# Selective scan with a gated MLP on one core: decay rows loaded at the head of two queues, B weighed by GpSimd in block 0, fewer and wider dummy matmuls

## The chip, the cores and the metric

The kernel runs on one core of a Trainium2 chip: TensorE (PE) for matmuls, VectorE (DVE), ScalarE (ACT) and GpSimd (POOL) for elementwise work, and SyncE (SP), which here only issues transfers; ACT issues some too. The metric is the device time of one execution in microseconds, as the median over runs. A profile is of one such execution; its span runs from the first to the last instruction.

## The reference, cut to what matters

```python
# x (4, 8, 768, 32), a (4, 8, 768) decays, B and C (4, 8, 768, 16)
log_a = np.log(np.clip(a, 1e-06, 1.0))
for c in range(nc):                      # chunks of the sequence
    cum = np.cumsum(la, axis=-1)
    L = np.exp(cum[:, :, :, None] - cum[:, :, None, :]) * causal
    y_intra = ((C @ B^T) * L) @ x
    y_inter = (C @ state) * np.exp(cum)[..., None]
    y[:, :, sl] = y_intra + y_inter
    state = decay_full * state + sum_j (B_j * decay_from_j) x_j
h = y as (3072, 256)
out = (silu(h @ w_gate) * (h @ w_val)) @ w_out      # d_ff = 1536
```

## The kernel before

The 768 steps of the sequence are cut into six blocks `k` of 128 steps, each of two pieces `q` of 64. A block holds all four batches `b`, so 512 tokens. In each block the scan part gives `y`, and the MLP part gives twelve gate and value products `gv` (one weight tile `wg0` to `wg11` each), then the sums `po` with `wo0` to `wo5`. The MLP's products are most of PE's work.

Products of decays within a piece are made by a scan along the free axis on DVE, which writes `L` (per source step) and `E` (per state). B is weighed by a column of `L` (`weigh_b`), C by `E` (`weigh_c`). `S` are the scores C B, `mix` multiplies them by `L`, `st` are the sums that make the new states, which ACT takes apart into `T`. `values` gives the first part of `y`, `carried` adds what comes from the state of the piece before.

Block 0 is the head. Its decays come as rows (`load_rows`): for the pieces, the partitions 32 b and 32 b + 1 of the tile `rows` hold batch `b`; 8 further rows hold the decays for `E`. `clip_rows` clips them, PE spreads a row over partitions by a matmul with a selector from `cs` (`spread`, output `a`, in two halves of the heads), and DVE scans that (`scan_spread`). The decays of the other blocks are loaded into `all`, clipped by POOL (`clip_all`), written back to memory as `clipped`, and read from there, broadcast, block by block. `dj` and `dn` are the added terms of the scans. `idle` issues dummy matmuls on the tile `unit`, with output `rest`.

Weights come as 64-bit words. DVE and ACT turn each tile into a float32 value (steps magnitude, range, rest, shift, sign, round) and then into a high and a low part. In block 0 `gv` uses the float32 values; in the others it uses the parts.

The order of instructions is not written out by hand: `Plan` is a small list scheduler. Each operation is added with an engine and a cost, a rank (its due time), what it needs, and the buffers it takes; `Plan.order` simulates the engines, and at each step issues what can start first, with the lowest rank. `follow` chains operations into a fixed order. Every engine runs its instructions strictly in the order issued. `IDLE` lists the ranks of five groups of dummies, `IDLE_AFTER` what each group follows. Transfers issued from SP and ACT are given eight completion semaphores in turn, so an issue can wait for an earlier transfer that had the same one.

All helpers that issue instructions pass through one line, 190, so the profile's lines say little, and the tile names are what to read.

Of the kernel before, what the change touches and what calls it, by code (L numbers as in the profile page):

```python
# [23 lines left out]
K = P // Q  # L24
# [19 lines left out]
class Plan:  # L44
# [156 lines left out]
def scan_moe_kernel(ctx: ExitStack, tc, aj, an, bc, xb, wgv, wo, cst, sel, out):  # L201
    nc = tc.nc
    PSUM = bass.MemoryType.PSUM
    te, ve, se, ge, sp = (
        Ordered(tc, e) for e in (nc.tensor, nc.vector, nc.scalar, nc.gpsimd, nc.sync)
    )
# [4 lines left out]
    const = pool("const", 1)  # L211
# [3 lines left out]
    raw = pool("raw", RAW)  # L215
    dram = pool("dram", 1, space=bass.MemoryType.DRAM)
    ps_mm = pool("ps_mm", 4, space=PSUM)
    ps_at = pool("ps_at", 4, space=PSUM)

    cs = const.tile([P, CST], F32, name="cs")  # L220
    eye, hm, blk = cs[:, 0:W], cs[:, W : W + 2], cs[:, W + 2 : W + 2 + 2 * D]
    pick = cs[:, CST - P :]
    dj = const.tile([P, H, W], F32, name="dj")
    dn = const.tile([P, BATCH * K, W], F32, name="dn")
    unit = const.tile([P, P], BF16, name="unit")
    pick_n = const.tile([H, P], F32, name="pick_n")

    const.tile([P, 48], F32, name="gap")
# [1 line left out]
    clipped = dram.tile([2, P, NA * W], F32, name="clipped")  # L230
    bl = [dict(y={}) for _ in range(NB)]
# [8 lines left out]
    def load_rows():  # L240

        t = moe.tile([P, 2, T + 32], F32, tag="xl", name="rows")
        t = bl[0]["rows"] = t[:, :, : H * W]
        ve.memset(t[:, 0], 1.0)
        to = t[:, 0].rearrange("(b r) c -> b r c", b=BATCH)
        for q in range(K):
            sp.dma_start(to[:, q], aj[0, q].rearrange("(b c) -> b c", b=BATCH))
        sp.dma_start(t[:H, 1], an[0])

    def load_aj(k):  # L250
# [34 lines left out]
    def load_xb(k):  # L285
        t = bl[k]["xb"] = att.tile([P, BATCH, DM + P], F32, tag="xb", name=f"xb{k}")
        bl[k]["x"], bl[k]["Bj"] = t[:, :, :DM], t[:, :, DM:]
        (sp if k else se).dma_start(t, xb[k])
# [11 lines left out]
        ve.tensor_tensor_scan(t, t, d, 0.0, ALU.mult, ALU.add)  # L300

    def clip_rows(i):
        t = bl[0]["rows"][:H, 1] if i else bl[0]["rows"][:, 0]
        clip(t.rearrange("p (g t) -> p g t", t=W)[:, :, 1:])

    HALF = H // 2 * W
# [1 line left out]
    def first(b, i):  # L308
        return b < BATCH and not i
# [37 lines left out]
            else:  # L347
                ve.tensor_scalar(t[:, :, h], bl[k]["C"], hm[:, h : h + 1], None, ALU.mult)

    def weigh_b(k, b):  # L350

        t = bl[k]["Bj"].rearrange("p b (h n) -> p b h n", n=N)[:, b]
        L = bl[k]["L"].rearrange("p (b h) t -> p b h t", h=H)[:, b, :, Q:]
        ve.tensor_tensor(out=t, in0=t, in1=L.to_broadcast([P, H, N]), op=ALU.mult)

    def weigh_c(k):
        t = bl[k]["C"].rearrange("p b (q i) -> p b q i", i=Q)
# [286 lines left out]
    ve.memset(unit, 1.0)
    se.dma_start(cs, cst)
    sp.dma_start(pick_n, sel)
    new_decays(0)
# [37 lines left out]

    for n, ranks in enumerate(IDLE):
        for i, r in enumerate(ranks):
            need = [("idle", n, i - 1)] if i else IDLE_AFTER[n]
            takes = [] if i else [("at", ("rest", n))]
            add("PE", 0.12, do(idle, n, i), r, need, takes=takes, uses=[("rest", n)], gives=("idle", n, i), kind="r")  # L690


    for i in range(NW):
        r = due(0, i) - 1.0 if i < NF else due_sum(0, 2 * (i - NF)) - 1.0
        add("SP", 0.48, do(w_fetch, i), r - 9.0, ["clipped"] if 2 <= i < 7 else [("y", 0)] if i == 7 else [], takes=[("raw", ("raw", i))], gives=("raw", i), lag=2.1)
        add([("Act", 0.6), ("DVE", 0.335)], None, do(w_magnitude, i), r - 5.5, [("raw", i)], takes=[("sg" if i < NF else "w", ("w", i))], gives=("mag", i))
# [17 lines left out]
    for k in range(NB):  # L714
        r = due(k)
        SLACK = min(k / 2, 1.0)
        z = -5 if not k else r + LEAD[min(k, 3)]
        L, E, BC, XB, CZ, TT = ("L", k), ("E", k), ("bc", k), ("xb", k), ("Cz", k), ("T", k)
# [6 lines left out]
        q = ("SP", 0.48) if k else ("-", 0.0)  # L725
# [6 lines left out]
        add(*q, load(load_xb), FETCH["xb"] if k == 1 else z - 6 if k else -6, late + behind("xb") + loaded, takes=[("xb", XB)], gives=("xb", k), lag=3.1)  # L732
        if not k:
            add("-", 0.0, lambda: None, -9, takes=[("x", "rows")], gives="rows", lag=0.2)
            for i in range(2):
                add("DVE", 0.35, do(clip_rows, i), -9 + i, ["rows"], gives=("clip", i))
            for b in range(BATCH + 1):
                r = z + 0.5 + b if b < BATCH else -1.3
                for i in range(2):
                    t = ("spread", b, i)  # L740
                    add("PE", 0.25 if first(b, i) else 0.45, do(spread, b, i), r + 0.5 * i, [("clip", b // BATCH), "pick" if b == BATCH else "cs"], takes=[("mm" if first(b, i) else "at", t)], uses=[t, "rows"], gives=t, kind="s")
                    need = [t, ("decays", 0), "dj"] + ([("scan0", b)] if i else [])
                    done = ("scan0", b) if not i else ("L", 0, b) if b < BATCH else ("E", 0)
                    add("DVE", 0.63, do(scan_spread, b, i), r + 0.5 * i, need, uses=[t], gives=done)
        else:
            add("SP", 0.96, do(load_aj, k), FETCH["aj"] if k == 1 else z - 12, ["written", ("decays", k), *late], gives=("aj", k), lag=4.3)
            add("SP", 0.48, do(load_an, k), FETCH["an"] if k == 1 else z - 9, ["written", ("decays", k), *late], gives=("an", k), lag=1.1)
            for b in range(BATCH):
                add("DVE", 1.14, do(scan_j, k, b), z + 0.5 + b, [("aj", k)], gives=("L", k, b), slack=1.0)
            add("DVE", 1.17, do(scan_n, k), z + 6, [("an", k)], gives=("E", k), slack=1.0)  # L750
        for b in range(BATCH):
            add("DVE", 0.21, do(weigh_b, k, b), z + 1.0 + b if k else -1.2, [("L", k, b), ("xb", k)], gives=("bt", k, b))
        add([("Act", 1.35), ("DVE", 0.72)], None, do(heads_apart, k), z, [("bc", k)], takes=[("Cz", CZ)], gives=("Cz", k))
        add("DVE", 0.6 if k else 0.35, do(weigh_c, k), z + 8 if k else -1.0, [("E", k), ("Cz", k)], gives=("ce", k))
        st = [("st", k, q) for q in range(K - last(k, K - 1))]
        S = [("S", k, p) for p in range(NP)]
# [32 lines left out]
            add("PE", 0.2, do(carried, 0, b), -1, [("vals", 0), ("vals", 1), ("ce", 0), *steps], uses=uses, gives=("y", 0) if b == BATCH - 1 else ("y", 0, b), kind="f")  # L789
        done = [("y", k)]  # L790
        if not k:
            add("-", 0.0, new_whole, -9, [("clip", 0), ("clip", 1)], takes=[("x", "xf")], gives="xf")
            for i in range(2 * K):
                add([("Act", 0.36), ("DVE", 0.36)], None, do(x_whole, i), z + 16 + i / 2, [*done, "xf"], uses=[y[i]], gives=("xf", i))
            continue
# [6 lines left out]
    for k in range(NB):  # L802
# [31 lines left out]
                add("SP", 0.48, do(store, k, m, t), r + 2, [o], uses=[o], gives=("stored", k, m, t), lag=0.9)  # L834
    halves = [(b, i) for i in range(2) for b in range(BATCH)]
    plan.follow([
        *(("spread", b, 0) for b in range(BATCH)), *(("idle", 1, i) for i in range(len(IDLE[1]))),
        *(("spread", b, 1) for b in range(BATCH)), *(("S", 0, b) for b in range(BATCH)),
        *(("spread", BATCH, i) for i in range(2)), *(("st", 0, b) for b in range(BATCH)), ("idle", 2, 0),
    ])  # L840
    plan.follow([("raw", i) for i in range(NW)])
    plan.follow([("L", 0, b) if i else ("scan0", b) for b, i in halves] + [("M", 0, p) for p in range(NP)] + [("scan0", BATCH), ("E", 0), ("ce", 0)])
# [2 lines left out]


CST = W + 2 + 2 * D + P
REST = 64
NA = NB * K * BATCH * H // P
IDLE = [-9.0] * 10, [-4.0] * 6, [-1.0 + 0.1 * i for i in range(3)], [-1.0 + 0.1 * i for i in range(4)], [0.5 + 0.5 * i for i in range(8)]  # L850
IDLE_AFTER = [], [("spread", BATCH - 1, 0)], [("S", 0, BATCH - 1)], [("vals", 1)], [("y", 0)]
FETCH = dict(aj=10.0, an=29.0, bc=12.0, xb=31.0)
LATER = 3.0
LEAD = {1: -30.0, 2: -44.0, 3: -44.0}
# [51 lines left out]
```

## Time and profile before

| | |
|---|---|
| median of 3 runs | 366.31 us (365.36 to 366.67) |
| the profiled execution | 366.59 us, span 364.8 us |
| PE busy | 350.5 us, 96% of the span |
| DVE busy | 238.3 us, 65% |
| ACT, POOL busy | 116.2 us, 2.3 us |
| mean granted clock of TensorE | 1.000 |
| read from memory, written | 24.33 MB, 3.35 MB |

A busy time is the union of an engine's instructions. "PE" are matmuls and "PEld" loads of the stationary operand, which overlap them. In rows of the timeline stand the start in us, the busy time, the engine, the operation, output and inputs by tile name, shapes, how many, and in brackets how long the engine had been idle before and what ended that.

### The profile page before, as it was taken

The numbers are of one execution on the slowest core, as the hardware profiler recorded it, in microseconds if no ns is written. First come the engines' busy times: TensorE is split into PE (matmuls) and PEld (weight loads), VectorE is DVE, ScalarE is ACT, GpSimd is POOL, SyncE is SP. The second block draws the span as 40 slices with busy tenths as digits, with TensorE's granted clock in tenths as the row PEclk, the third lists the DMA queues.
The fourth block names the chain that finished last, engine by engine and source line by source line (L and its number), as shares of the span: only waits on it lengthen the run. The fifth ranks groups of instructions, "written<-read, shape, count | busy, mean of one in ns | idle before, by whom it ended". The sixth has DMA issues, their size and how long they took to land.

```text
span 364.8 us, 7565 instructions
## 1 busy us (share of the span) xinstructions
PE 350.5 (96%) x3284; PEld 269.5 (74%) x3284; DVE 238.3 (65%) x446; ACT 116.2 (32%) x210; POOL 2.3 (1%) x7
## 2 busy tenths in 40 slices
PE   2969999999999999999999999999999999999996
PEld 2664444568886788887788887788887788888895
DVE  1858999989999879368264868266668251366230
ACT  3148657632344350222130222130222130221221
POOL 1100000000000000000000000000000000000000
PEclk9999999999999999999999999999999999999999
DMA  6828961182000056100038100037100000100001
GB/s 243 276 98 212 358 234 63 61 229 62 0 2 2 2 177 172 59 0 3 2 109 182 61 0 2 4 113 178 58 0 2 4 0 2 58 0 2 0 0 59
DMA packets 8457, 28.16 MB, mean 77 GB/s; under 512 B 976, under 2 KB 1880, under 8 KB 7784
## 3 DMA queue, kind: packets, MB, share of 16 engines
q1 hardware_dynamic: 7992, 26.23, 23.8%
q10 hardware_dynamic: 432, 1.44, 1.1%
q8 instruction: 26, 0.43, 0.5%
q14 instruction: 7, 0.06, 0.0%
HBM read 24.33 MB, written 3.35 MB: 76 GB/s over the span
## 4 chain that ended last, share of the span: by engine, by line
PE 76%; DVE 14%; DMA 5%; issue 4%; ACT 0%; SPq 0%; DVEq 0%; ACTq 0%
PE gv L190 40%; PE po L190 27%; PE y L190 4%; DVE sg L190 3%; DVE L L190 3%; DMA L<-clipped 3%; PE S L190 2%; PE rest L190 1%; PE a L190 1%; DMA rows<-in_aj 1%; PE st L190 1%; DMA wg0r<-in_wgv 1%; DVE T L190 1%; DVE wo1w L190 1%; DVE wg9w L190 1%
## 5 line engine op out<-in xcount | busy, mean ns | idle before, releaser
L190 DVE TENSOR_TENSOR sg<-gv,sg 128x512 f32<-128x512 f32 x72 | 49.5, 688 | 76.2 <-PE gv L190 74.8
L190 ACT ACTIVATE sg<-gv 128x512 f32<-128x512 f32 x72 | 42.9, 596 | 108.3 <-PE gv L190 108.2
L190 DVE TENSOR_TENSOR hh<-sg,hh 128x512 fp32r<-128x512 f32 x72 | 49.5, 691 | 14.2 <-ACT hh L190 12.9
L190 ACT CAST hh<-sg 128x512 fp32r<-128x512 f32 x41 | 25.4, 622 | 45.3 <-PE po L190 15.6
L190 DVE TENSOR_TENSOR_SCAN L<-L,dj 128x520 f32<-128x520 f32 x20 | 23.8, 1227 | 7.1 <-DMA L<-clipped 7.1
L190 ACT COPY ob<-po 128x512 f32<-128x512 f32 (+1 forms) x13 | 7.2, 555 | 48.7 <-PE po L190 48.2
L190 PE MATMUL po<-hh,wo0h 128*128 128x512 f32 (+1 forms) x52 | 15.7, 385 | 0.0
L190 DVE TENSOR_TENSOR L<-S,L 128x512 f32<-128x512 f32 x24 | 15.2, 681 | 0.5 <-PE S L190 0.5
L190 PE MATMUL po<-hh,wo5h 128*128 128x512 f32 (+1 forms) x52 | 15.2, 375 | 0.0
L190 PE MATMUL po<-hh,wo2h 128*128 128x512 f32 (+1 forms) x52 | 15.2, 375 | 0.0
L190 PE MATMUL po<-hh,wo3h 128*128 128x512 f32 (+1 forms) x52 | 15.2, 375 | 0.0
L190 PE MATMUL po<-hh,wo4h 128*128 128x512 f32 (+1 forms) x52 | 15.1, 373 | 0.0
L190 PE MATMUL po<-hh,wo1h 128*128 128x512 f32 (+1 forms) x52 | 15.0, 373 | 0.0
L190 PEld LDWEIGHTS y<-L,xb 64*32 64x32 f32 x768 | 9.3, 111 | 6.6 <-issue 5.4
L190 DVE CAST hh<-sg 128x512 fp32r<-128x512 f32 x31 | 13.2, 427 | 1.0
L190 PE MATMUL y<-L,xb 64*32 64x64 f32 x768 | 11.6, 239 | 1.9 <-issue 1.9
L190 PEld LDWEIGHTS po<-hh,wo4h 128*128 128x128 f32 x52 | 9.5, 188 | 1.7
L190 PEld LDWEIGHTS po<-hh,wo1h 128*128 128x128 f32 x52 | 9.5, 188 | 1.7
L190 PEld LDWEIGHTS po<-hh,wo3h 128*128 128x128 f32 x52 | 9.4, 188 | 1.8
L190 PEld LDWEIGHTS po<-hh,wo2h 128*128 128x128 f32 x52 | 9.4, 188 | 1.8
L190 PEld LDWEIGHTS po<-hh,wo5h 128*128 128x128 f32 x52 | 9.4, 188 | 1.7
L190 PEld LDWEIGHTS po<-hh,wo0h 128*128 128x128 f32 x52 | 9.2, 188 | 1.9 <-issue 0.2
(275 smaller groups left out, 718.2 us busy)
## 6 DMA issues: line engine op xcount, KB each, us to landing
L<-clipped SPq DMA_DIRECT2D x10, 520.0 KB, 7.3
xb<-in_xb SPq DMA_DIRECT2D x5, 768.0 KB, 14.7
out<-ob SPq DMA_DIRECT2D x11, 256.0 KB, 2.0
bc<-in_bc SPq DMA_DIRECT2D x5, 512.0 KB, 3.6
E<-clipped SPq DMA_DIRECT2D x5, 260.0 KB
xb<-in_xb ACTq DMA_DIRECT2D x1, 768.0 KB, 5.9
bc<-in_bc ACTq DMA_DIRECT2D x1, 512.0 KB
wg0r<-in_wgv SPq DMA_DIRECT2D x1, 512.0 KB
```

Source lines behind the costliest of these rows:

```text
L190: ins = getattr(self.engine, name)(*a, **k)
```

## The change

- The tile `rows` is not filled with ones any more, and its two transfers of `a` go one to SP's queue and one to ACT's, each as the first.
- `clip_rows` clips per batch (two partitions) instead of all 128 partitions at once; each spread needs only its batch's clip.
- In block 0 B is weighed by POOL instead of DVE.
- `unit` is 512 columns wide (POOL fills the added 384). The first group of dummies has 8 times 4 narrow matmuls instead of 10 times 4; the group between the two halves of the spreads is gone; the later groups have 3, 3 and 4 matmuls of 512 columns instead of 3, 4 and 8 times 4 of 64 columns.
- wg5 and wg6 need the first mix of block 0 in the plan, where they needed the clip of `all`.

```diff
-        ve.memset(t[:, 0], 1.0)
...
-            sp.dma_start(to[:, q], aj[0, q].rearrange("(b c) -> b c", b=BATCH))
+            (se if q else sp).dma_start(to[:, q], aj[0, q].rearrange("(b c) -> b c", b=BATCH))
...
-        t = bl[0]["rows"][:H, 1] if i else bl[0]["rows"][:, 0]
+        t = bl[0]["rows"]
+        t = t[:H, 1] if i == BATCH else t[32 * i : 32 * i + K, 0]
...
-    def weigh_b(k, b):
+    def weigh_b(k, b, e=ve):
...
-        ve.tensor_tensor(out=t, in0=t, in1=L.to_broadcast([P, H, N]), op=ALU.mult)
+        e.tensor_tensor(out=t, in0=t, in1=L.to_broadcast([P, H, N]), op=ALU.mult)
...
-        for _ in range(4):
-            te.matmul(rest[n][:, :REST], unit, unit[:, :REST], start=True, stop=True)
+        times, wide = (4, 64) if not n else (1, 512)
+        for _ in range(times):
+            te.matmul(rest[n][:, :wide], unit[:, :P], unit[:, :wide], start=True, stop=True)
...
+    ge.memset(unit[:, P:], 1.0)
...
-            for i in range(2):
-                add("DVE", 0.35, do(clip_rows, i), -9 + i, ["rows"], gives=("clip", i))
+            for i in range(BATCH + 1):
+                add("DVE", 0.32, do(clip_rows, i), -9 + 0.1 * i, ["rows"], gives=("clip", i))
...
-IDLE = [-9.0] * 10, [-4.0] * 6, [-1.0 + 0.1 * i for i in range(3)], [-1.0 + 0.1 * i for i in range(4)], [0.5 + 0.5 * i for i in range(8)]
+IDLE = [-9.0] * 8, [-1.0 + 0.1 * i for i in range(3)], [-1.0 + 0.1 * i for i in range(3)], [0.5 + 0.5 * i for i in range(4)]
```

What it does to the order on ACT's queue at the head of the program: first before, then now (`xb` is x and B of block 0, `bc` is B and C by states).

```order
L190 DMA cs<-in_cst 128x259
L190 ACT_TABLE_LOAD
L190 ACTIVATE warm<-warm 128x1
L190 DMA bc_99<-in_bc 128x1024
L190 DMA xb_101<-in_xb 128x1536
L190 COPY dj<-cs 128x520
```

```order
L190 DMA rows<-in_aj 4x520
L190 DMA cs<-in_cst 128x259
L190 ACT_TABLE_LOAD
L190 ACTIVATE warm<-warm 128x1
L190 DMA bc_98<-in_bc 128x1024
L190 DMA xb_100<-in_xb 128x1536
L190 COPY dj<-cs 128x520
```

A transfer of `rows` now stands ahead of `cs`, and the issue of `xb` shares its completion semaphore with a transfer of `rows`.

On POOL, from the fills of constants to the clip of `all`, before:

```order
L895 MEMSET const-uint8-127 128x1
L190 MEMSET dn 128x520
L190 MEMSET dn 128x8
L190 ISA
L190 TENSOR_SCALAR all<-all 128x6x64
```

and now:

```order
L190 MEMSET unit 128x384
L190 MEMSET dn 128x520
L190 MEMSET dn 128x8
L190 ISA
L190 TENSOR_TENSOR xb_100<-xb_100,L_94 128x128 x2
L190 TENSOR_SCALAR all<-all 128x6x64
L190 TENSOR_TENSOR xb_100<-xb_100,L_94 128x128 x2
```

Two of the four weighings of B stand ahead of the clip of `all`, two behind it.

On DVE, from the last scans of block 0's `L` to its mixes, before:

```order
L190 SCALAR_TENSOR_TENSOR L_95<-a_1_203,dj 128x260
L190 TENSOR_TENSOR xb_101<-xb_101,L_95 128x128 x3
L190 SCALAR_TENSOR_TENSOR L_95<-a_1_206,dj 128x260
L190 TENSOR_TENSOR L_95<-S_0_209,L_95 128x4x2x64
L190 TENSOR_TENSOR L_95<-S_1_210,L_95 128x4x2x64
L190 TENSOR_TENSOR xb_101<-xb_101,L_95 128x128
```

and now:

```order
L190 SCALAR_TENSOR_TENSOR L_94<-a_1_172,dj 128x260
L190 SCALAR_TENSOR_TENSOR L_94<-a_1_175,dj 128x260
L190 TENSOR_TENSOR L_94<-S_0_178,L_94 128x4x2x64
L190 TENSOR_TENSOR L_94<-S_1_179,L_94 128x4x2x64
L190 TENSOR_TENSOR L_94<-S_2_180,L_94 128x4x2x64
```

The four weighings of `xb` have left DVE; the mixes follow the scans directly.

More of the change, by code (lines that the diff above doesn't have):

```diff
@@ L224, in scan_moe_kernel @@
     dn = const.tile([P, BATCH * K, W], F32, name="dn")
-    unit = const.tile([P, P], BF16, name="unit")
+    unit = const.tile([P, 512], BF16, name="unit")
     pick_n = const.tile([H, P], F32, name="pick_n")
@@ L636, in idle @@
         if not i:
-            rest[n] = ps_at.tile([P, P], F32, tag="at", name=f"rest{n}")
-        for _ in range(4):
-            te.matmul(rest[n][:, :REST], unit, unit[:, :REST], start=True, stop=True)
+            rest[n] = ps_at.tile([P, 512], F32, tag="at", name=f"rest{n}")
+        times, wide = (4, 64) if not n else (1, 512)
+        for _ in range(times):
+            te.matmul(rest[n][:, :wide], unit[:, :P], unit[:, :wide], start=True, stop=True)
     warm = const.tile([P, 1], F32, name="warm")
     load_rows()
-    ve.memset(unit, 1.0)
+    ve.memset(unit[:, :P], 1.0)
     se.dma_start(cs, cst)
@@ L689, in scan_moe_kernel @@
             takes = [] if i else [("at", ("rest", n))]
-            add("PE", 0.12, do(idle, n, i), r, need, takes=takes, uses=[("rest", n)], gives=("idle", n, i), kind="r")
+            add("PE", 0.22, do(idle, n, i), r, need, takes=takes, uses=[("rest", n)], gives=("idle", n, i), kind="r")
     for i in range(NW):
         r = due(0, i) - 1.0 if i < NF else due_sum(0, 2 * (i - NF)) - 1.0
-        add("SP", 0.48, do(w_fetch, i), r - 9.0, ["clipped"] if 2 <= i < 7 else [("y", 0)] if i == 7 else [], takes=[("raw", ("raw", i))], gives=("raw", i), lag=2.1)
+        add("SP", 0.48, do(w_fetch, i), r - 9.0, ["clipped"] if 2 <= i < 5 else [("M", 0, 0)] if 5 <= i < 7 else [("y", 0)] if i == 7 else [], takes=[("raw", ("raw", i))], gives=("raw", i), lag=2.1)
         add([("Act", 0.6), ("DVE", 0.335)], None, do(w_magnitude, i), r - 5.5, [("raw", i)], takes=[("sg" if i < NF else "w", ("w", i))], gives=("mag", i))
@@ L740, in scan_moe_kernel @@
                     t = ("spread", b, i)
-                    add("PE", 0.25 if first(b, i) else 0.45, do(spread, b, i), r + 0.5 * i, [("clip", b // BATCH), "pick" if b == BATCH else "cs"], takes=[("mm" if first(b, i) else "at", t)], uses=[t, "rows"], gives=t, kind="s")
+                    add("PE", 0.25 if first(b, i) else 0.45, do(spread, b, i), r + 0.5 * i, [("clip", b), "pick" if b == BATCH else "cs"], takes=[("mm" if first(b, i) else "at", t)], uses=[t, "rows"], gives=t, kind="s")
                     need = [t, ("decays", 0), "dj"] + ([("scan0", b)] if i else [])
@@ L751, in scan_moe_kernel @@
         for b in range(BATCH):
-            add("DVE", 0.21, do(weigh_b, k, b), z + 1.0 + b if k else -1.2, [("L", k, b), ("xb", k)], gives=("bt", k, b))
+            add("DVE" if k else "Pool", 0.21 if k else 0.4, do(weigh_b, k, b) if k else do(weigh_b, 0, b, ge), z + 1.0 + b if k else -1.2, [("L", k, b), ("xb", k)], gives=("bt", k, b))
         add([("Act", 1.35), ("DVE", 0.72)], None, do(heads_apart, k), z, [("bc", k)], takes=[("Cz", CZ)], gives=("Cz", k))
@@ L791, in scan_moe_kernel @@
         if not k:
-            add("-", 0.0, new_whole, -9, [("clip", 0), ("clip", 1)], takes=[("x", "xf")], gives="xf")
+            add("-", 0.0, new_whole, -9, [("clip", BATCH)], takes=[("x", "xf")], gives="xf")
             for i in range(2 * K):
@@ L836, in scan_moe_kernel @@
     plan.follow([
-        *(("spread", b, 0) for b in range(BATCH)), *(("idle", 1, i) for i in range(len(IDLE[1]))),
+        *(("spread", b, 0) for b in range(BATCH)),
         *(("spread", b, 1) for b in range(BATCH)), *(("S", 0, b) for b in range(BATCH)),
-        *(("spread", BATCH, i) for i in range(2)), *(("st", 0, b) for b in range(BATCH)), ("idle", 2, 0),
+        *(("spread", BATCH, i) for i in range(2)), *(("st", 0, b) for b in range(BATCH)), ("idle", 1, 0),
     ])
@@ L847 @@
 CST = W + 2 + 2 * D + P
-REST = 64
 NA = NB * K * BATCH * H // P
-IDLE = [-9.0] * 10, [-4.0] * 6, [-1.0 + 0.1 * i for i in range(3)], [-1.0 + 0.1 * i for i in range(4)], [0.5 + 0.5 * i for i in range(8)]
-IDLE_AFTER = [], [("spread", BATCH - 1, 0)], [("S", 0, BATCH - 1)], [("vals", 1)], [("y", 0)]
+IDLE = [-9.0] * 8, [-1.0 + 0.1 * i for i in range(3)], [-1.0 + 0.1 * i for i in range(3)], [0.5 + 0.5 * i for i in range(4)]
+IDLE_AFTER = [], [("S", 0, BATCH - 1)], [("vals", 1)], [("y", 0)]
 FETCH = dict(aj=10.0, an=29.0, bc=12.0, xb=31.0)
```

## The prediction

> **What bounds the kernel now.** I read the page first, for the share of each engine and for the stretches in which TensorE (PE) is not busy; then the chain of waits, for where the first gate product starts; then the timeline of the first 32 us, since the diff touches nothing later; last some stretches, to see who could hold back what moves forward.
>
> The page, and rows of the chain (start, duration, what):
>
> ```profile
> PE 350.5 (96%) x3284; PEld 269.5 (74%) x3284; DVE 238.3 (65%) x446; ACT 116.2 (32%) x210; POOL 2.3 (1%) x7
> ...
> q8 instruction: 26, 0.43, 0.5%
> ```
> ```profile
> 1.43 4.02 DMA rows<-in_aj
> ...
> 17.89 1.89 issue
> 19.78 0.78 PE y L190 x36
> ...
> 22.37 1.42 issue
> ```
>
> PE is idle 14.3 of 364.8 us, most of it before `gv` starts. From there PE is the bound with VectorE (DVE) close behind. In the stretches (duration, then busy time of each engine) PE works almost all the time, and DVE all of it from 45 to 70:
>
> ```profile
> 19.80:22.40 2.60, 2.57 (x128) 2.23 (x128) 1.20 (x3) 1.49 (x5) 0.00 (x0) 1.00 0.22 85
> ...
> 31.00:45.00 14.00, 14.00 (x34) 6.27 (x33) 13.23 (x24) 10.72 (x21) 0.00 (x0) 1.00 0.99 287
> 45.00:60.00 15.00, 15.00 (x159) 7.01 (x158) 15.00 (x34) 10.16 (x20) 0.00 (x0) 1.00 0.52 197
> 60.00:70.00 10.00, 9.17 (x146) 4.51 (x145) 10.00 (x19) 6.47 (x12) 0.00 (x0) 1.00 0.16 54
> ```
>
> So what counts is how much earlier the first `gv` starts (27.68), and whether weights, DVE and transfers follow. The head, from the timeline (start, busy us, engine, what, [idle before <- who ended it]):
>
> ```profile
> 0.73 0.38 ACTq L190 DMA_DIRECT2D cs<-in_cst  x1
> ...
> 0.91 0.49 DVE L190 MEMSET rows<- 128x520 f32 x1 [0.91 <-PEq L895]
> ...
> 1.43 1.28 SPq L190 DMA_DIRECT2D rows<-in_aj  x2
> ...
> 1.61 0.33 ACTq L190 DMA_DIRECT2D bc<-in_bc  x1
> 1.98 0.45 ACTq L190 DMA_DIRECT2D xb<-in_xb  x1
> ...
> 5.47 1.33 ACT L190 ACTIVATE Cz<-bc,cs 128x512 f32<-128x512 f32 x2 [1.98 <-DMA bc<-in_bc]
> ...
> 8.25 0.75 DVE L190 TENSOR_SCALAR rows<-rows 128x512 f32<-128x512 f32 x2 [6.69 <-DMA rows<-in_aj]
> ...
> 8.73 1.25 PE L190 MATMUL a<-rows,cs 2*128 2x260 f32 x8 [4.81 <-DMA wg0r<-in_wgv]
> 8.93 1.49 POOL L190 TENSOR_SCALAR all<-all 128x384 f32<-128x384 f32 x1 [7.50 <-DMA all<-in_an]
> ...
> 10.06 4.38 DVE L190 TENSOR_TENSOR_SCAN L<-a,dj 128x260 f32<-128x260 f32 x7 [1.07 <-PE a L190]
> ...
> 12.59 2.01 PE L190 MATMUL S<-Cz,bc 32*64 32x128 f32 x64
> 12.84 0.73 SPq L190 DMA_DIRECT2D wg6r<-in_wgv  x1
> ...
> 14.37 0.67 DVE L190 TENSOR_TENSOR xb<-xb,L 128x128 f32<-128x128 f32 x3
> ```
> ```profile
> 16.74 0.28 DVE L190 TENSOR_TENSOR xb<-xb,L 128x128 f32<-128x128 f32 x1
> 16.94 1.28 DVE L190 TENSOR_TENSOR L<-S,L 128x512 f32<-128x512 f32 x2
> ...
> 20.59 1.18 PE L190 MATMUL y<-L,xb 64*32 64x64 f32 x59
> ...
> 21.71 0.66 PE L190 MATMUL rest<-unit 128*128 128x64 bf16 x9
> ...
> 22.63 0.43 DVE L190 TENSOR_SCALAR wg1w<-wg1w 128x512 f32<-128x512 f32 x1 [1.62 <-ACT wg1w L190]
> ...
> 23.79 1.20 PE L190 MATMUL rest<-unit 128*128 128x64 bf16 x19 [1.42 <-issue]
> 24.91 1.13 PE L190 MATMUL y<-bc,T 32*64 32x64 f32 x32
> 25.98 1.89 PE L190 MATMUL rest<-unit 128*128 128x64 bf16 x32
> 26.10 0.37 ACT L190 COPY xf<-y 128x256 f32<-128x256 f32 x1 [2.69 <-PE y L190]
> 26.14 0.42 DVE L190 COPY xf<-y 128x256 f32<-128x256 f32 x1 [2.15 <-PE y L190]
> ...
> 27.68 3.98 PE L190 MATMUL gv<-xf,wg0w 128*128 128x512 f32 x8
> ...
> 31.76 0.69 DVE L190 TENSOR_TENSOR sg<-gv,sg 128x512 f32<-128x512 f32 x1 [1.27 <-PE gv L190]
> ```
>
> DVE sat 6.7 us on the two small transfers of decays, and everything in block 0 hangs on the clip at 8.25.
>
> **The rows.** Before, SP issues them after the fill (1.43), the second from about 2.1, behind `bc` and `xb`, which ScalarE's queue (ACT) had issued from 1.61. The transfers issued, with their time to landing:
>
> ```profile
> xb<-in_xb ACTq DMA_DIRECT2D x1, 768.0 KB, 5.9
> ...
> wg6r<-in_wgv SPq DMA_DIRECT2D x1, 512.0 KB, 9.2
> cs<-in_cst ACTq DMA_DIRECT2D x1, 129.5 KB, 2.1
> ```
>
> `xb` landed at 1.98 + 5.9 = 7.9, and the clip could start at 8.25: the second small transfer waited out the large ones. Now one row transfer stands first on each queue, about 0.73, where `cs` stood. Nearest prices: 2.1 (`cs`, first in its queue) and 4.02 (first row transfer, `bc` beside it). I take 2.1, since nothing large is ahead of either: landed at 2.9; the other end is 4.75. `cs` moves behind a row issue of 1.28 / 2 = 0.64 us: issued at 1.4, landed at 3.5, and the spreads `a` need it. So `a` starts near 3.6, against 8.73: **5.1 earlier**. The five clips of about 0.38 (half of the 0.75) run from 2.9 to 4.8, one ahead of each spread, and are covered by the scans behind them. The fill of `rows` (0.49) is gone from a path that held SP. The larger fill of `unit` puts 384 columns on GpSimd (POOL), idle until 8.9 before: free. On ACT `bc` slips by 0.1 to 0.4, and `xb` now waits for a row transfer to land (about 2.9 for 1.98), one us late, with `dj` and `Cz` queued behind that issue; `dj` needs `cs` anyway.
>
> **The scans.** From `a` to the first scan stays 10.06 - 8.73 = 1.33: first scan at 4.9. From there to the last mix took 18.22 - 10.06 = 8.16, of which 0.80 was weighing B (four at about 0.2 each) and goes to POOL. 8.16 - 0.80 = 7.36: last mix done at 12.3 for 18.22. `S` needs `Cz` (6.8 before, 7.2 at most now) and the banks of four scans (4.9 + 4 x 0.62 = 7.4), takes 2.0, done at 9.4, before the last scan: covered.
>
> **B on POOL.** `st`, and behind it on PE all of `y`, now wait for POOL. On POOL two weighings stand before the clip of `all` and two behind it; on SP the write of `clipped` and wg2 to wg6 queue behind that clip.
>
> No two-input operation of POOL is in the trace. Bounds: 0.2 (what DVE needs), and 1.0 (twice a third of the 1.49, for two inputs). I take the third alone, 0.5, nearest to POOL's own row. `xb` is in by about 8.5 (7.9 plus part of its us); then 9.0, 9.5, clip to 11.0, 11.5, 12.0; `st` of the last batch and `y` follow at 12.4. With 0.2, `y` starts at 11.5; with 1.0 at 14.2. [...]
>
> **From y to gv.** 59 `y` took 1.18 us, so 128 take 2.5: 12.4 to 14.9 (last mix 12.3, no wait). Dummies: 28 + 32 = 60 narrow ones went (0.66 + 1.20 + 1.89 = 3.75), 10 wide ones come: six, then the carried part, then four. A narrow one is 0.059 for 64 columns; eight times that is 0.47, the upper bound. But the carried `y` at 24.91 took 35 ns a matmul, and this one, the same shape in block 1, 18:
>
> ```profile
> 63.12 3.70 PE L190 MATMUL gv<-xf,wg9w 128*128 128x512 f32 x8 [0.83 <-DVE wg9w L190]
> ...
> 71.17 1.16 PE L190 MATMUL y<-bc,T 32*64 32x64 f32 x64
> ```
>
> PE runs at half pace in the head, so the lower bound is half, 0.23. PE is busy without a break from 12.4, so I take 0.35 for the six (2.1) and 0.27 for the four (1.1). 14.9 + 2.1 + 1.0 (carried) + 1.1 = 19.1. `xf` is ready at 18.0 + two copies on ACT of 0.37 = 18.8, inside that. The 24 dummies between the spreads, and eight of the first forty, cost nothing and bring nothing: PE waited there for DVE and for the rows.
>
> **The two issue stalls** (1.89 and 1.42) are instruction fetch, by the rows: 26 pieces of 0.43 MB in all are 256 instructions of 64 B each, PE has 3284 + 3284 = 25.7 x 256, and between the two stalls stand 128 matmuls and 128 loads. Counting its instructions, a piece ended in `y` and one in the dummies behind; with 700 instead of 864 ahead of `gv` the ends fall in `y` (after 82 of its 256, about 13.2) and at the first `gv`. From entering a piece to having the next took 23.79 - 19.78 = 4.0 with idle transfers, about 6.9 with loaded ones (13.0 to 19.78). The first is then ready before `y` needs it: 1.9 saved. The second would be ready at 17.2 to 20.1: I add 0.3 of a wait. [...]
>
> **The sum.** `gv` starts at 19.1 + 0.3 = 19.4 for 27.68: 8.3 earlier. DVE must follow: its mixes end 5.9 earlier, its idle times of 1.62, 2.15 and 1.27 can shrink by up to 5.0, three low-part scalings (wg0r, wg2r, wg3r) come over from ACT and one copy leaves, net two of about 0.42. 5.9 + 5.0 - 0.8 = 10.1 is more than 8.3, with 1.8 of idle to spare. Transfers: wg6 landed at 12.84 + 9.2 = 22.0; its queue starts 0.6 later, with the backlog ahead of it shorter, so block 1's loads follow about 7.5 earlier. I give back 0.3. **8.0 us off**: the profiled run's 366.59 (1.79 outside its span) goes to 358.6; the median shown, 366.31, is 0.28 below that run, so 358.5.
>
> **Rivals.** (1) POOL becomes the wait: 1.0 a weighing, `y` at 14.2, 1.8 lost, 360.3. For it: no row of such an operation; against: POOL's fills and clip are quick. (2) Both fetches stall as before, with the weights' transfers beside them: 8.0 - 1.9 - 1.1 = 5.0, 361.5. For it: the first stall was the longer one, beside full queues. (3) The clock: `gv` starts at half pace. Its first eight took 3.98 where wg9's took 3.70: 0.3 is the least. If wg0's eight all ran at half pace it would be 3.7, and I take half of that, 1.8: 360.3. For it: half pace throughout the head; against: fuller dummies, and PE busy without a break from 12.4 on. [...] (4) The change does not do what it says: the rows still land near 8, and only the 0.8 of B, the dummies and a stall come off: 364.0. Against it: nothing large is ahead of them. (5) Slower: the clip of `all` now waits on POOL for `xb` and two scans, and wg2 to wg6 behind it. By my sum the clip ends 0.6 later than before and wg2 is issued about 11.9; even at wg6's 9.2 it lands at 21. Its `gv` is due at 19.4 + 2 x 3.7 = 26.8, less some 3 us of preparation: 23.8. Each us past that is a us lost; at 33.8 the kernel is slower, 368.5. For it: POOL keeps its order; against: `xb` was in at 7.9.
>
> **Numbers.** Forecast (357.3 to 359.7) 0.52; (1) 0.16; (2) 0.13; (3) 0.12; (4) 0.04; (5) 0.03. The range 356.8 to 361.8 reaches below for weighings of 0.2 with dummies of 0.23, and above for (2). 0.5% (1.8 us) is about what a measurement of this kernel can tell from no change: faster 0.94, same 0.03, slower 0.03.
>
> **What would show it.** First `a` near 3.6, first scan near 4.9, last mix near 12.3, first `y` near 12.4 released by POOL, at most one issue stall before `gv`, first `gv` near 19.4. Wrong if the clip starts after 5, POOL's weighing is over 1 us, or if DVE idles and PE waits for wg2 to wg9 by more than the 0.83 of before.

## The result and the profile after

The changed kernel takes 362.03 us (359.01 to 363.12) beside 365.56 us (365.36 to 366.67) for the kernel before, each a median of five runs: ratio 0.9882, interval 0.9834 to 0.9929. It is faster, by 3.5 us of the 7.8 forecast. The median lies 0.2 above the stated range of 356.8 to 361.8; two of the five runs lie in it. The profiled execution took 362.03 us with a span of 360.2, 4.6 below the 364.8 of before.

The page of the changed kernel, the rows that answer to those of before:

```profile
PE 348.1 (97%) x3202; PEld 265.8 (74%) x3202; DVE 238.9 (66%) x445; ACT 115.0 (32%) x209; POOL 4.3 (1%) x12
...
q8 instruction: 25, 0.41, 0.5%
```

The chain of waits to the first gate product, in order of time (start, duration, what), is now another one. Before, it ran from the rows through DVE's scans to `y`; now it runs through the transfer of `xb` and POOL:

```profile
0.73 2.26 DMA rows<-in_aj
...
3.02 8.10 DMA xb<-in_xb
...
11.26 0.04 POOL xb L190
...
12.13 1.49 POOL all L190
...
13.70 0.47 POOL xb L190
...
14.21 0.84 PE st L190 x32
15.05 2.03 PE y L190 x124
17.08 1.60 PE rest L190 x6
18.68 0.62 PE y L190 x32
19.30 0.75 PE rest L190 x3
20.05 2.15 issue
...
22.59 1.72 PE gv L190 x4
```

The timeline of the head (start, busy us, engine, what, idle before and who ended it):

```profile
0.73 1.08 ACTq L190 DMA_DIRECT2D rows<-in_aj  x1
...
1.85 0.35 ACTq L190 DMA_DIRECT2D cs<-in_cst  x1
...
3.11 2.21 DVE L190 TENSOR_SCALAR rows<-rows 2x512 f32<-2x512 f32 x5 [2.11 <-DMA rows<-in_aj]
3.40 0.42 SPq L190 DMA_DIRECT2D wg0r<-in_wgv  x1
...
4.03 0.34 SPq L190 DMA_DIRECT2D wg1r<-in_wgv  x1
...
4.15 2.88 PE L190 MATMUL a<-rows,cs 2*128 2x260 f32 x16 [1.21 <-DMA cs<-in_cst]
5.45 4.83 DVE L190 TENSOR_TENSOR_SCAN L<-a,dj 128x260 f32<-128x260 f32 x8
...
7.70 2.27 PE L190 MATMUL S<-Cz,bc 32*64 32x128 f32 x64 [0.67 <-ACT Cz L190]
...
10.20 2.46 DVE L190 TENSOR_TENSOR L<-S,L 128x512 f32<-128x512 f32 x4
11.26 0.79 POOL L190 TENSOR_TENSOR xb<-xb,L 128x128 f32<-128x128 f32 x2 [9.47 <-DMA xb<-in_xb]
...
13.70 0.83 POOL L190 TENSOR_TENSOR xb<-xb,L 128x128 f32<-128x128 f32 x2
...
14.21 0.84 PE L190 MATMUL st<-xb 64*32 64x64 f32 x32 [1.61 <-POOL xb L190]
...
14.80 2.28 PE L190 MATMUL y<-L,xb 64*32 64x64 f32 x128
...
22.20 0.39 PE L190 MATMUL rest<-unit 128*128 128x512 bf16 x1 [2.15 <-issue]
```

The first scan is 4.6 us earlier (5.45 for 10.06) and the last mix 5.6 (12.65 for 18.22). At the first `gv`, 22.43 for 27.68, 5.25 are left, and 4.6 at the end. So something is lost twice: between the mix and `y`, where PE waits for POOL, and ahead of `gv`, where PE waits for its own instructions (a fetch stall, `issue` in the rows: 2.15 from 20.05, while a packet of 16,384 B on the instruction queue q8 ran from 19.74 to 20.73). What PE waited for over the whole span (total, times, longest), before and then after:

```profile
PE y L190 <- issue: 1.9, 1, 1.9
...
PE rest L190 <- issue: 1.4, 1, 1.4
PE gv L190 <- DVE wg9w L190: 0.8, 1, 0.8
PE S L190 <- DVE T L190: 0.6, 1, 0.6
```
```profile
PE rest L190 <- issue: 2.2, 1, 2.2
PE st L190 <- POOL xb L190: 1.6, 1, 1.6
PE S L190 <- DVE T L190: 1.3, 1, 1.3
...
PE gv L190 <- DVE wg9w L190: 0.9, 1, 0.9
```

Two fetch stalls of 3.3 became one of 2.15. The wait at `wg9` is as before. The wait for `S` of block 2, at 107, is 0.7 longer: that is the rest of the difference between 5.25 and 4.6.

### The profile page after: what moved, and what is told of

The parts are those of the page before. It is cut to its first block, busy times and chain, and to the rows that moved or that the text cites. A ratio compares the mean times of both kernels' runs of the same rounds, so it can differ in the third digit from the quotient of the medians.

```text
span 360.2 us, 7405 instructions
## 1 busy us (share of the span) xinstructions
PE 348.1 (97%) x3202; PEld 265.8 (74%) x3202; DVE 238.9 (66%) x445; ACT 115.0 (32%) x209; POOL 4.3 (1%) x12
## 4 chain that ended last, share of the span: by engine, by line
PE 75%; DVE 12%; DMA 6%; issue 4%; ACT 1%; SPq 1%; POOL 1%; POOLq 0%; DVEq 0%; ACTq 0%
PE gv L190 40%; PE po L190 27%; DMA xb<-in_xb 6%; PE y L190 4%; DVE sg L190 2%; DVE L L190 2%; PE S L190 1%; PE st L190 1%; PE rest L190 1%; SPq L190 1%; DMA rows<-in_aj 1%; DVE wg5w L190 1%; DVE wg8w L190 1%; DVE wo1w L190 1%; DVE wg9w L190 1%
## 5 line engine op out<-in xcount | busy, mean ns | idle before, releaser
L190 DVE TENSOR_TENSOR hh<-sg,hh 128x512 fp32r<-128x512 f32 x72 | 49.5, 691 | 13.7 <-ACT hh L190 12.3
L190 PEld LDWEIGHTS S<-Cz,bc 32*64 32x64 f32 x384 | 6.9, 144 | 5.2 <-issue 2.2
```

What stands on the lines that cost most here:

```text
L190: ins = getattr(self.engine, name)(*a, **k)
```

## The experiments

The theory after the result had three terms. (a) POOL holds `y` back not through its pace: `xb` lands late, and the clip of `all` (1.49) then stands between the weighings. (b) The stall ahead of `gv` is the fetch of a piece of 256 instructions, and where its border falls decides what it costs. (c) Part of an earlier `gv` is lost again in block 2. The rivals: POOL's pace, a slowing of the fetch by the weights' transfers, and the clock. All ratios are to the kernel before.

| kernel | time, us | ratio, interval | last packet of `xb` | first `y` | first `gv` | fetch stall ahead of it | wait at `S`, block 2 |
| --- | --- | --- | --- | --- | --- | --- | --- |
| kernel before | 365.56 | 1 | 7.3 | 17.20 | 27.68 | 1.89 in `y`, 1.42 | 0.6 |
| changed kernel | 362.03 | 0.9882, 0.9834 to 0.9929 | 10.8 | 14.80 | 22.43 | 2.15 | 1.3 |
| e1: rows alone | 362.97 | 0.9925, 0.9901 to 0.9948 | 9.3 | 13.39 | 24.31 | 4.01 | none |
| e10: dummies alone | 364.98 | 0.9969, 0.9944 to 0.9993 | 7.2 | 16.68 | 24.78 | 1.31 in `y` | 0.5 |
| e2: B on VectorE | 360.42 | 0.9842, 0.9814 to 0.9871 | 8.1 | 12.48 | 20.10 | 1.41 | 1.3 |
| e3: `xb` on SP's queue | 361.31 | 0.9880, 0.9857 to 0.9903 | other queue | 12.84 | 20.57 | 1.26 | 1.4 |
| e4: clip first | 360.08 | 0.9839, 0.9807 to 0.9871 | 8.1 | 12.29 | 19.84 | 1.75 | 1.0 |
| e5: no first dummies | 357.93 | 0.9779, 0.9756 to 0.9802 | 10.4 | 12.45 | 20.48 | none | 0.4 |
| e6: weights later | 362.86 | 0.9918, 0.9892 to 0.9943 | 8.3 | 12.69 | 19.90 | 1.47 | 1.3 |
| e8: e4 and e5 | 359.33 | 0.9805, 0.9775 to 0.9834 | 10.5 | 12.10 | 20.11 | 0.79 in `y` | 0.6 |
| e9: e2 and e5 | 357.45 | 0.9780, 0.9755 to 0.9805 | 8.9 | 12.60 | 19.36 | 0.17 in `y` | 0.7 |
| e11: e4, no dummies at all | 359.40 | 0.9836, 0.9808 to 0.9863 | 9.6 | 12.59 | 18.77 | 1.43 in `y` | none |
| e12: e3, e4 and e5 | 358.04 | 0.9808, 0.9773 to 0.9844 | other queue | 12.10 | 18.58 | none | none |

The last five columns are from one profiled execution each ("none": no such wait over 0.25 us). The last packet of `xb` is the last on ACT's transfer queue in the trace; POOL could start 0.4 to 0.6 us after it. Runs of one kernel lie up to 4.4 us apart (e12), so differences of a microsecond between two rows are not told apart by these times.

**Rows alone (e1)**: the kernel before with the edits of `rows` only.

```diff
-        ve.memset(t[:, 0], 1.0)
...
-            sp.dma_start(to[:, q], aj[0, q].rearrange("(b c) -> b c", b=BATCH))
+            (se if q else sp).dma_start(to[:, q], aj[0, q].rearrange("(b c) -> b c", b=BATCH))
```

> The kernel before with the rows' part of the change alone: no fill, one row transfer at the head of each queue, clips by batch. B stays on VectorE, the dummies stay narrow. My theory (x and B of block 0, the tile xb, now land at about 11 us instead of 7.9, and all that weighs B waits for it): the first scan starts at about 5.4 instead of 10.1, but VectorE then stands at the weighing of B until xb lands at 11.1, the last mix ends near 14.9 for 18.2, both issue stalls stay, the first gv starts near 24.3; time about 362.3. Rival (the rows bring all of the 5 us that they start earlier, xb is no limit): last mix near 13.6, first gv near 23, time about 361.

Measured 362.97 us, 2.8 below before. `a` starts at 4.21 and the first scan at 5.52, so the rows' part of the head is what the changed kernel has. But PE's chain then shows a stall that ate half of it:

```profile
15.69 0.72 PE rest L190 x9
16.41 4.01 issue
20.43 1.20 PE rest L190 x19
```

The instructions are those of before. The piece behind the border 698 instructions in was had 6.7 us after the border at 442 was passed (13.69, by counting loads in the trace), and with an earlier head there is less work to wait beside. The first `gv` came where it was expected, but not for the reason given: DVE weighed B from 10.55 without a wait for `xb`, whose last packet had ended at 9.3.

**Dummies alone (e10)**: the kernel before with the new `IDLE`, the wide `unit` and no group between the spreads.

```diff
-IDLE = [-9.0] * 10, [-4.0] * 6, [-1.0 + 0.1 * i for i in range(3)], [-1.0 + 0.1 * i for i in range(4)], [0.5 + 0.5 * i for i in range(8)]
+IDLE = [-9.0] * 8, [-1.0 + 0.1 * i for i in range(3)], [-1.0 + 0.1 * i for i in range(3)], [0.5 + 0.5 * i for i in range(4)]
```

> The kernel before with only the dummies changed: 8 instead of 10 groups at the start, none between the spreads, and 3, 3 and 4 wide ones in place of 15 groups of 4 narrow ones. Theory (dummies and the borders of the fetch): the head up to y is as before (first scan 10.0, last mix 18.2, y from 17.2); PE issues 164 instructions fewer ahead of gv; y, six dummies 1.6, the carried part 0.6 and 0.3 of dummies, with 0 to 3 us of stalls: gv at 22.0 to 25.0 for 27.68, time 1.5 to 4 us below the kernel before. Rival (clock): ten dummies are too few, the first eight gv take over 4.5 us for 3.98, and the gain is under 1 us. Second rival (fetch stalls keep their 3.3 us in all): gv at 25.0 or later, gain at most 2 us.

Measured 364.98 us (361.95 to 366.32), 1.05 below before: less than expected. The profiled execution, 363.03, is among the lowest of its runs, so its `gv` at 24.78, inside the expected span, is a favourable one. With e1's 2.8, the two parts alone make 3.8 of the 5.3 that both together gain (e2, beside the same runs of before as e1); the intervals allow that they just add.

**B on VectorE (e2)**: the changed kernel without the move to POOL.

```diff
-            add("DVE" if k else "Pool", 0.21 if k else 0.4, do(weigh_b, k, b) if k else do(weigh_b, 0, b, ge), z + 1.0 + b if k else -1.2, [("L", k, b), ("xb", k)], gives=("bt", k, b))
+            add("DVE", 0.21, do(weigh_b, k, b), z + 1.0 + b if k else -1.2, [("L", k, b), ("xb", k)], gives=("bt", k, b))
```

> The changed kernel with B of block 0 weighed on VectorE again. My theory (xb's landing near 11.1 is the wait, whoever weighs): VectorE waits there, last mix near 14.9 (12.7 in the changed kernel), first y near 13.5 to 14.5 (14.7), first gv within 0.7 of the changed kernel's 22.4; time within 1 us of it, 361 to 363. Rival (GpSimd is slow, and its clip stands in the way): first y near 12.4 and about 2 us gained, 360.

Measured 360.42 us: the medians are 1.6 below the changed kernel, the intervals overlap. In the profile the last mix ends 0.7 later (13.38), the clip of `all` runs at once (8.75), `y` starts at 12.48 and `gv` 2.3 earlier. No gain of 0.8 from the move to POOL is seen. The expectation, that `xb` is the wait whoever weighs, was missed, and this run can't test it: `xb`'s last packet had ended at 8.1, 2.7 earlier than in the changed kernel's profile.

**`xb` on SP's queue (e3)**, ahead of `all` and wg0.

```diff
-        (sp if k else se).dma_start(t, xb[k])
+        sp.dma_start(t, xb[k])
```

> The changed kernel with the load of xb on SyncE's queue behind the rows and the selector, ahead of the copies of the decays and wg0, wg1, so that it does not wait for a row transfer's semaphore and nothing large is ahead of it but bc. My theory: xb lands near 8 to 8.5, GpSimd starts at about 8.6 instead of 11.3, first y near 12.4 instead of 14.7, first gv near 20.2; time about 2 us below the changed kernel's, near 360. Rival (the clip of all on GpSimd between the weighings is the wait, since it then waits for all, now landing later): first y stays near 14, time within 0.7 of the changed kernel's. Second rival (fetch of TensorE's instructions sets the start of gv): first y comes earlier but gv stays near 22.

Measured 361.31 us. `xb` landed at 7.75 instead of 11.12, POOL weighed as soon as DVE's scans allowed, and `y` began at 12.84:

```profile
8.64 0.42 POOL L190 TENSOR_TENSOR xb<-xb,L 128x128 f32<-128x128 f32 x1 [6.86 <-DVE L L190]
9.23 0.41 POOL L190 TENSOR_TENSOR xb<-xb,L 128x128 f32<-128x128 f32 x1 [0.17 <-DVE L L190]
9.73 1.49 POOL L190 TENSOR_SCALAR all<-all 128x384 f32<-128x384 f32 x1
11.30 0.78 POOL L190 TENSOR_TENSOR xb<-xb,L 128x128 f32<-128x128 f32 x2
```

So POOL needs 0.4 a weighing and is no bound; the late `xb` was. The time moved by 0.7 only, where 2 were expected, and that is under what these runs resolve.

**Clip first (e4)**: POOL clips `all` before it weighs.

```diff
-[("L", k, b), ("xb", k)], gives=("bt", k, b))
+[("L", k, b), ("xb", k)] + ([] if k else ["clipped"]), gives=("bt", k, b))
```

> The changed kernel with the clip of all ahead of the four weighings of B on GpSimd. My theory (xb's landing sets the first weighing at 11.3, and the clip's 1.5 us between the second and the third is the rest of the delay): weighings end near 12.9 instead of 14.5 and first y of the second half no later than 13.2; gv 1 to 1.6 earlier if the fetch of instructions allows, but the weights' transfers then start 2 us earlier and load the queues while TensorE fetches, so the issue stall before gv stays 2 us or grows; time 0 to 1.5 below the changed kernel's. Rival (the clip in between costs nothing, the stall alone sets gv): time within 0.3 of the changed kernel's, gv at 22.4.

Measured 360.08 us; the clip ran from 8.83, the weighings from 10.40 to 11.92, `y` from 12.29, which is the 12.4 of the prediction. Here too `xb` was in early (last packet at 8.1), so it did not set the first weighing, as had been expected. With `y` on time there is still a fetch stall:

```profile
19.41 0.59 PE L190 MATMUL rest<-unit 128*128 128x512 bf16 x2 [1.75 <-issue]
```

In e2, e3 and e4 `gv` comes 1.9 to 2.6 earlier. But in all three `xb` was in early, and in e6 below, with `xb`'s queue and POOL's order as in the changed kernel, it was too and `gv` came 2.5 earlier. So these three profiles do not separate the edits from an early `xb`; e6 and e8 together do.

**No first dummies (e5)**: 32 matmuls and 32 loads fewer at the very start. The plan then also puts three weighings ahead of the clip on POOL, where the changed kernel has two.

```diff
-IDLE = [-9.0] * 8, [-1.0 + 0.1 * i for i in range(3)], [-1.0 + 0.1 * i for i in range(3)], [0.5 + 0.5 * i for i in range(4)]
+IDLE = [], [-1.0 + 0.1 * i for i in range(3)], [-1.0 + 0.1 * i for i in range(3)], [0.5 + 0.5 * i for i in range(4)]
```

> The changed kernel without its first group of dummies (32 matmuls and 32 loads at the very start, where TensorE waits for the decays anyway). No operation of the critical path changes; every later instruction of TensorE only stands 64 places earlier in its program. Theory (the 2.15 us stall ahead of the first gv is the fetch of a piece of 256 instructions that begins 698 instructions in, two before gv): the border now falls 62 instructions into gv, which are reached some 14 us later, so that stall vanishes; the border before it (442) falls in the middle of y, and may wait 0 to 1 us there. First gv at 20.3 to 21.3 for 22.43, time 0.5 to 2 us below the changed kernel's. Rival (the stall is a wait for something else, the transfers or a semaphore): it stays ahead of gv, gv at 22.4, time unchanged. Second rival (the first dummies warm TensorE): S and y are slower, S over 2.3 us and y over 2.5 us.

Measured 357.93 us, ratio 0.9779, clear of the changed kernel's interval: 4.1 us by the medians (1.0% in ratio), beyond the 0.5 to 2 expected. The profiled span is 2.9 shorter than the changed kernel's, 1.95 of it at `gv` and 0.9 at `S` of block 2. What PE waited for:

```profile
PE a L190 <- DVE rows L190: 4.0, 1, 4.0
PE gv L190 <- DVE wg9w L190: 0.9, 1, 0.9
PE st L190 <- POOL xb L190: 0.7, 1, 0.7
...
PE S L190 <- DVE T L190: 0.4, 1, 0.4
```

No wait on issue over 0.25 us is left. POOL's last weighing still ends at 14.31, but only that one is late, so `y` starts at 12.45 and waits 0.7 in its middle. The border stands at the same count, 442 and 698, but other work stands there: 698 is now in `gv` of wg3, long after it is fetched. The stall ahead of `gv` is gone in all five kernels without the first group (e5, e8, e9, e11, e12), and all six that have that group and the early rows (the changed one, e1 to e4, e6) have one: that shows (b), as to where PE stalls. What the removal is worth in time is less clear: 1.0% in ratio to before here, 0.6% in e9 beside e2, but 0.3% in e8 beside e4, with overlapping intervals. The other side: the six dummies took 2.74 for 1.67 and the carried part 0.85 for 0.69, so PE's pace in the head did fall, but `S` (2.15 us) did not slow, and the first eight `gv` took 3.60 as in the changed kernel. Of the second rival, slower `S` and `y`, no more than that is seen.

**Weights later (e6)**: wg4 to wg6 are issued once the first part of `y` is done.

```diff
-["clipped"] if 2 <= i < 5 else [("M", 0, 0)] if 5 <= i < 7 else [("y", 0)] if i == 7 else []
+["clipped"] if 2 <= i < 4 else [("y", 0)] if 4 <= i < 8 else []
```

> The changed kernel with the loads of wg4 to wg6 held on SP's queue until the first part of y of block 0 is done, so that fewer weights travel while TensorE's next piece of instructions is fetched (entered near 15.4, had at 22.2: 6.8 us, where 4.0 was seen with idle transfers). Theory (the weights' transfers slow the fetch): the 2.15 us stall ahead of gv falls to 0 to 0.8, gv at 20.3 to 21.1, time 0.5 to 1.5 us lower. Rival (the latency is the fetch's own, whatever travels): the stall stays near 2, gv at 22.4, time the same. Price that would hide a gain: wg4 to wg6 land late and TensorE waits for them with the first-block gv 4 to 6 (due 14.8 us and more after the first gv).

Measured 362.86 us, no gain. The fetch was no quicker: the border at 442 was passed at 13.22 and the next piece had at 19.67, 6.4 us for 6.9, and wg4 came late:

```profile
PE gv L190 <- DVE wg4w L190: 1.8, 1, 1.8
PE rest L190 <- issue: 1.5, 1, 1.5
```

wg2, wg3 and the head's own transfers were still in flight, so this does not clear the transfers. In this execution POOL's first weighing began at 8.87, `xb` being there 2.3 us earlier than in the changed kernel's profile, with the same issues ahead of it: its landing varies from one execution to the next, which may be much of the spread of the runs. With POOL's order unchanged, `y` then starts at 12.69 and `gv` at 19.90:

```profile
8.87 0.78 POOL L190 TENSOR_TENSOR xb<-xb,L 128x128 f32<-128x128 f32 x2 [7.08 <-DMA xb<-in_xb]
9.74 1.49 POOL L190 TENSOR_SCALAR all<-all 128x384 f32<-128x384 f32 x1
11.30 0.78 POOL L190 TENSOR_TENSOR xb<-xb,L 128x128 f32<-128x128 f32 x2
```

**Clip first and no first dummies (e8)**: the edits of e4 and e5 together.

> Two edits on the changed kernel: GpSimd clips all decays ahead of its four weighings of B, and the first group of dummies is gone. Clip first alone had gv at 19.84 with a stall of 1.75 ahead of it. If that stall is the fetch and its border moves into gv, gv starts at 18.1 to 18.9 and the time is 358.5 to 359.8; if the stall merely moves to y in full, gv stays near 19.8 and the time near 360. A rival on the gain's way into the time: what is won ahead of gv is given back at the scores S of block 2 (PE's wait there 1.0 to 1.4 in the kernels with an early gv, 0.6 before), so the span falls by less than half of what gv gains.

Measured 359.33 us, in the expected band, with `gv` at 20.11, which is later than expected. The stall moved into `y` and shrank (0.79), but six dummies took 2.43 us. The third rival is not borne out: the wait at `S` is 0.6 with a `gv` this early. This profile also answers (a), for here `xb` was late (last packet at 10.5), and with the clip first `y` still starts at 12.10:

```profile
9.52 1.49 POOL L190 TENSOR_SCALAR all<-all 128x384 f32<-128x384 f32 x1 [7.73 <-DMA all<-in_an]
11.08 1.53 POOL L190 TENSOR_TENSOR xb<-xb,L 128x128 f32<-128x128 f32 x4
```

With an early `xb` and the clip in between (e6) it is 12.69, and with both a late `xb` and the clip in between (the changed kernel) 14.80. So it takes the two together to hold `y` back, by one profiled execution of each.

**No dummies at all (e11)**: clip first as in e4, and

```diff
-IDLE = [-9.0] * 8, [-1.0 + 0.1 * i for i in range(3)], [-1.0 + 0.1 * i for i in range(3)], [0.5 + 0.5 * i for i in range(4)]
+IDLE = [], [], [], []
```

> GpSimd clips ahead of its weighings, and no dummy matmuls at all, neither at the start nor around the carried part of y. With clip first and without the first group, y ended at 16.3, six dummies took 2.4 us, the carried part ended at 19.3 and gv began at 20.11. Theory (the dummies only stand in the way): the carried part follows y at once (its T is ready at 15.5), the second copy of xf 0.4 us behind it, gv at 17.7 to 18.5; the first eight gv take 3.4 to 3.8 us as before; time 1.5 to 2.2 us below that kernel, 356.8 to 358.2. Rival (the clock: the dummies buy the full pace for gv): gv starts at about 18 too, but the first eight take 5 us or more, and the time is 359 or more.

Measured 359.40 us, against the theory and for the rival, `gv` at half pace:

```profile
18.77 6.40 PE L190 MATMUL gv<-xf,wg0w 128*128 128x512 f32 x8 [0.62 <-DVE xf L190]
25.01 3.60 PE L190 MATMUL gv<-xf,wg1w 128*128 128x512 f32 x8
```

`gv` starts 1.3 earlier than in e8, and the second eight start 1.5 later (25.01 for 23.54). The dummies cost 1.3 us ahead of `gv` and buy 2.8 in it; the medians of the two kernels (359.40 and 359.33) don't tell them apart.

**`xb` on SP, clip first, no first dummies (e12)**, the edits of e3, e4 and e5, and **B on VectorE, no first dummies (e9)**, those of e2 and e5.

> Clip first, no first group of dummies, and xb issued on SP's queue ahead of the decays' large tile and wg0 (there it landed at 7.75 for 11.1). Theory (with the clip first, the weighings start when it ends, about 10.4 to 11.0, and xb is no wait any more): weighings 10.4 to 12.0, y from 12.1 to 16.0 with the border's stall of 0.5 to 1.0 inside it, gv at 19.4 to 20.3, time within 0.7 us of the kernel without the xb edit (359.33). Rival (fewer transfers in flight speed the fetch): the stall in y is gone, gv at 18.9 to 19.4, time 0.5 to 1 us lower.

> B weighed by VectorE as before the change, and no first group of dummies. Theory (which engine weighs B is worth little once the fetch's border is out of the way): weighings by VectorE 9.5 to 12.2, last mix 13.4, y 12.5 to 15.5 with 0 to 1 us of stall in it, dummies 2.4 to 2.7, gv at 19.4 to 20.5, time 357.3 to 359.5, as with GpSimd (357.93). Rival (GpSimd is what saves): last mix 0.8 later than with GpSimd shows in full, gv 0.8 later, time 0.7 us or more above.

e12: 358.04 us (356.85 to 361.26). `gv` at 18.58, the earliest with full pace, and no issue stall over 0.25: the stall in `y` is gone, as the rival said. That fewer transfers made the fetch quicker is not shown, and the time (1.3 lower, intervals overlapping) does not decide. e9: 357.45 us with `gv` at 19.36, the lowest median of all, not told apart from e5's 357.93. With the border moved, it does not show which engine weighs B. All three beat the kernel before; the intervals of e9 and e5 also lie clear of the changed kernel's, that of e12 overlaps it a little.

## Why the prediction was half right

The direction and the place were right, the amount was not: `gv` 8.3 earlier was forecast, 5.25 came. The terms in their order:

- **Rows.** Landed at 2.99 (2.9 forecast). `a` started at 4.15 for 3.6: the issue of the row transfer on ACT took 1.08, not 0.64, so `cs`, for which PE waited 1.21, was issued at 1.85 for 1.4. Lost: 0.55. Rival (4) is excluded, and e1 shows the part by itself.
- **Scans and mixes.** From first scan to last mix 7.20 for 7.36; the mix ended at 12.65 for 12.3. As forecast.
- **`xb` in by about 8.5** is the first step that failed. It landed at 11.12 in the profiled execution: the 5.9 of before became 8.10. Before, SP issued wg0 and wg1 at 5.47 and 8.12, behind waits for its earlier transfers; now they follow `xb` (3.02) at 3.40 and 4.03, and the sum left that out. Whether it made `xb` late is not shown: e2 and e4 issued the same transfers within 0.1 us of these times, and there `xb`'s last packet ended 5.2 after its issue, as before (5.3), not 7.7. In nine executions with these issues it ended at 8.1 to 10.8; in part, then, the miss is the luck of one execution, and what sets the landing stays open. The price of a weighing, 0.5, was too high: 0.42 in e3's single rows, 0.79 for two here. The clip between the weighings was in the sum; with `xb` late it came behind `xb` too, and `y` started at 14.80 for 12.4. With `xb` early and the same order (e6) it was 12.69. Lost: 2.4, more than rival (1) gave POOL, by another mechanism.
- **`y`, dummies, carried part.** 2.28 for 2.5, 1.60 for 2.1, 0.62 for 1.0: won back about 1.2 with the last dummies. The stated bounds (0.23 to 0.47 a dummy) held: the six took 0.27 each, the three behind the carried part 0.25. The choice of 0.35 and 0.27 between them was an estimate.
- **The fetch stall of 0.3** is the second step that failed: 2.15. The mechanism was right: q8 brought 25 pieces, 0.41 MB in all, for 6404 loads and matmuls, 256 a piece, and the stall stood at the border at 698, just ahead of `gv`. The size was taken too near the 4.0 of before, where the DMA share was 0.22 (19.80 to 22.40); here it was 0.90 (14.80 to 17.00) and 1.01 (19.80 to 22.40). The working had 6.9 too, from a stretch of before with a share of 1.01 (13.00 to 19.78), by which the piece is ready at 20.1 and PE waits 1.0; and 6.9 it was (border 442 passed at 15.3, piece had at 22.2), 6.2 in e4 and 6.7 in e1. The other 1.15 of the stall is what `y`, the dummies and the carried part had won back: PE came to the border the sooner. In e4, where `y` was on time, 1.75 was still lost. Rival (2) was half of what happened: of the two stalls one went. As to the pair 442 and 698: the packet with the next piece began 4.4 us after the border at 442 was passed (15.31), and 1.6 after it (19.78) in the kernel before.
- **Clock.** Rival (3) did not happen, the first eight `gv` took 3.60. e11 shows that it would have without the dummies: 6.40, beside 3.60 in e8, which has the wide ones.
- **Weights and DVE.** The wait at wg9 was 0.86 for 0.83, so DVE followed, and wg2 to wg6, issued at 14.08 and later for 11.9 forecast, were still in time: rival (5) did not happen.
- **Given back: 0.3 forecast, 0.7 measured** (5.25 at `gv`, 4.6 at the end), at `S` of block 2. There DVE waited for block 2's transfers, which it did not before:

```profile
DVE xb L190 <- DMA xb<-in_xb: 1.2, 1, 1.2
DVE L L190 <- DMA L<-clipped: 0.7, 1, 0.7
```

In the profiles this wait of DVE (0.9 in e5, 1.2 in e8, 1.9 here, 2.2 in e4, 2.7 in e6, 3.1 in e2) and PE's wait at `S` (0.4, 0.6, 1.3, 1.0, 1.3, 1.3) go roughly together. Others do not fit: before waited 0.6 at `S` and e9 0.7, with none and 0.3 of DVE's wait, and e12 did not wait at `S` with 0.8 of it. Why the transfers are later in some was not tried and stays open.

In sum: the 0.55 of the rows is covered by PE's wait for POOL, and `gv` came 8.3 - (2.4 + 1.85 - 1.2) = 5.25 earlier; then 0.7 was given back instead of 0.3.

## What to carry to other kernels

Count where the borders of PE's instruction fetch fall before you price dummies or anything else ahead of a dense stretch: 64 instructions that cost nothing where they stood put a stall of 2.15 us ahead of `gv` by where they pushed a border. When a transfer that held a queue is moved, list everything queued behind it, since that can start earlier too (here wg0 and wg1 were issued at 3.40 and 4.03 for 5.47 and 8.12). Before you put a late landing down to that, or an early one to your edit, look at the same transfer in several executions: here it ended anywhere from 8.1 to 10.8 with the same issues. And an operation moved to an idle engine has to fit that engine's order: what stands between its pieces (here 1.49 for the clip) can count more than its pace (0.4).

## What the hardware showed that was not expected

- The time from passing a border to having the next piece was 6.2 to 7.0 us in the six kernels e1 to e4, e6 and the changed one, with weights in flight, against 4.0 for the second of before. By the packets of queue q8, the 16 KB themselves took 0.9 to 1.0 us each time and PE went on 1.3 to 1.5 us after; the difference lies ahead of them, for they began 3.8 to 4.7 us after the border, against 1.6. It hardly shrank when three weights were held back (6.4, e6), and for the border at 186 it was 2.8 to 3.6 us in e8, e11 and e12, where wg2 to wg4 were issued at that time. What sets it is not settled.
- The granted clock in the profile's rows reads 1.00 throughout the head, also in e11 from 18.80 to 25.00, while the starts of the matmuls show half pace: the first six `gv` matmuls of e11 begin about 0.85 apart, later ones 0.43. The pace rose about 5.4 us after `gv` began (at 24.2); what sets that time these runs do not show.
- The landing of one and the same transfer, `xb` with the same issues ahead of it, was at or before 8.87 in e6 and at 11.12 in the changed kernel. Its last packet ended at 8.1 in e2 and e4, 8.3 in e6, 8.9 in e9, 9.3 in e1, 9.6 in e11, 10.4 in e5, 10.5 in e8 and 10.8 in the changed kernel.
